# Silu order, late queries and 72-row keys and values in an attention and feed-forward kernel

## The chip, the cores and the metric

The kernel runs on one core of a Trainium2 chip. Its time is the device time of one execution in microseconds; the median of ten runs stands for a kernel. A profile is of one execution, and its times count from the start of that execution's span.

## What is computed

Eight batches of attention with pooled keys and values, then a feed-forward layer with silu over all 4608 rows:

```
k_p = k.reshape(B, H, Sp, 8, D).mean(axis=3)      # B=8, H=8, Sp=72, D=64
v_p = v.reshape(B, H, Sp, 8, D).mean(axis=3)
attn = softmax(q @ k_p.T / sqrt(D))               # q has 576 rows for each head
x = (attn @ v_p) as 4608 rows of 512
h = x @ w_in                                      # 512 x 2048
out = (h * sigmoid(h)) @ w_out                    # 2048 x 512
```

## The kernel before

The loop at L788 walks over nine tiles t of 512 rows. Each tile has a first product, `up` (x by w_in, with silu into `h_T`), and a second one: `down` for tile 0, `down_quarters` for the others. The attention of batch a = t + 1 is laid between the matmuls of tile t, so that PE always has work.

What is laid where is written by hand. `spread` (L417) counts the steps of a product and runs a list of fillers, each due at a step; `f_up` and `f_down` are the lists of the two products. A filler's instructions take their place in each engine's queue at that moment, and every engine runs its queue in order. DMAs are issued in three queues: SP (output stores and the first half of each later key and value load), POOL (weights, queries, and loads that cast or add), and ACT (a few at the start and the end).

**Tiles 1 to 8** make both products with fewer multiplications: seven products of quarter matrices instead of eight. In `up` this is done for two units of four column groups (`UNITS`, L428), the rest being plain (`plain`, L537). `stage` (L502) does one product of a unit: product 2 goes into PSUM bank P and is copied by ACT to `r_sb` (L505); product 5 goes into Q and DVE adds `r_sb` (L508, `rr_sb`); product 1 goes into R and gives `t_sb` (L511); products 4 and 3 add into P and Q and ACT takes their silu; products 7 and 6 add into P and Q, DVE adds `t_sb` to make `c_sb` 0 and 1 (L520, L524), and ACT takes their silu (L496). "s" in an item stands for the silu of `c_sb` 1, and that of `c_sb` 0 follows product 7 directly (L521). The order of units is the string in `items`. A plain group goes through three PSUM banks with the tag mm. In `down_quarters` the sums of quarters of `h_T` are made by DVE (`hidden_sum`, L611) into five tiles `h_sum`, and those of `w_out` into `w_sum` (`weight_sum`, L629, in tiles 0 and 1).

**Keys and values** come in two ways. For batches 0 to 2 the 576 rows of a batch (8 heads by 72 positions, each of 8 by 64 numbers) lie in 128 rows by slots of 128 (`load_slots`, L251). `slot_sums` (L269) adds the eight parts on DVE; since a head's 72 rows then straddle slots, PE puts them in place by selection matmuls (`select_k` L289, `select_v` L305: 24 for keys and 12 for values of a batch), and `copy_k` and `copy_v` take them out of PSUM. Batch 2 is loaded in two halves, the second added by the DMA. From batch 3 on, keys and values lie in 72 rows with the heads side by side: `load_one` (L175, SP) loads one half, `load_rest` (L181, POOL) adds the other, `pool_k` (L199) and `pool_v` (L211) add up on DVE (L188, L193), and `k_transpose` (L217) turns the keys with four transposes on PE and one copy on ACT.

**Queries** are loaded by POOL (`load_q`, L129): one DMA for a batch, but eight of 144 KB for the last batch. `q_transpose` (L150) turns them on DVE. `scores`, `denominators` and `numerators` (L343 to L408) are the attention itself; `numerators` needs the values `vp`.

Of the kernel before, what the change touches and what calls it, by code (L numbers as in the profile page):

```python
# [27 lines left out]
FP32 = mybir.dt.float32  # L28
# [8 lines left out]
def kernel(  # L37
# [9 lines left out]
    nc = tc.nc  # L47
# [43 lines left out]
    def ps_tile(shape, dtype, tag, name):  # L91
# [12 lines left out]

    h_sum = {
        n: singles.tile([128, KQ, NQ], BF16, name=f"h_sum{n}") for n in (1, 2, 5, 6, 7)
    }
    o_sb = [singles.tile([128, 2, d_model], FP32, name=f"o_sb{n}") for n in range(2)]
# [65 lines left out]

    def load_one(b, name):  # L175
        st = batches.setdefault(b, {})
        raw = raw_tile(f"{name}_raw", H)
        load_rows(nc.sync, raw, source(b, name)[:, :, :PH])
        st[f"{name}_raw"] = raw

    def load_rest(b, name):  # L181
# [5 lines left out]
    def add_halves(raw):  # L187
        nc.vector.tensor_add(  # L188
            out=raw[:, :, : 2 * D], in0=raw[:, :, : 2 * D], in1=raw[:, :, 2 * D :]
        )  # L190
# [59 lines left out]

    def load_slots(eng, b, name, i0, i1, half=None):  # L251
        es = slice(0, RE) if half is None else slice(half * RE // 2, (half + 1) * RE // 2)
        src = (k if name == "k" else v)[b].rearrange("h (sp p) d -> (h sp) (p d)", p=POOL)
        src = src[:, es]
        how = dict(accum_op=ALU.add) if half else {}
        tiles = row_tiles[name]
        w = es.stop - es.start
        if i0 == SLOTS:
            eng.dma_start(
                out=tiles[1][:REST, SLOTS - SA, :w], in_=src[128 * SLOTS :], **how  # L260
            )
        else:
            j = i0 // SA
            eng.dma_start(
                out=tiles[j][:, i0 - SA * j : i1 - SA * j, :w],
                in_=src[128 * i0 : 128 * i1].rearrange("(i r) e -> r i e", r=128), **how
            )

    def slot_sums(name, j, halves=False):  # L269
        raw = row_tiles[name][j]  # L270
        dst = rows5[name][:, SA:] if j else rows5[name][:, :SA]
        w = RE // 4 if halves else RE // 2
        while w > D:
            nc.vector.tensor_add(  # L274
                out=raw[..., :w], in0=raw[..., :w], in1=raw[..., w : 2 * w]
            )
            w //= 2
        nc.vector.tensor_add(out=dst, in0=raw[..., :D], in1=raw[..., D : 2 * D])
# [192 lines left out]
    def up(t, fillers, items):  # L471
        step = spread(
            fillers,
            sum(
                KF if len(it) == 3 else 2 * len(it[1].strip("s")) for it in items
            ),
# [25 lines left out]
        def stage(y, n):  # L502
# [3 lines left out]
            elif n == "5":  # L506
                product(y, 5, "Q", True)
                tt(out=rr_sb, in0=ps["Q"], in1=r_sb, op=ALU.add)  # L508
            elif n == "1":
                product(y, 1, "R", True)  # L510
                tt(out=t_sb, in0=ps["R"], in1=rr_sb, op=ALU.subtract)  # L511
            elif n == "4":
                product(y, 4, "P", False)
                hidden(y, 1, 0, ps["P"])
            elif n == "3":
                product(y, 3, "Q", False)
                hidden(y, 0, 1, ps["Q"])
            elif n == "7":
                product(y, 7, "P", False)
                tt(out=c_sb[0], in0=ps["P"], in1=t_sb, op=ALU.add)  # L520
                hidden(y, 0, 0, c_sb[0])  # L521
            elif n == "6":
                product(y, 6, "Q", False)
                tt(out=c_sb[1], in0=ps["Q"], in1=t_sb, op=ALU.add)  # L524
            else:
                hidden(y, 1, 1, c_sb[1])
# [243 lines left out]
    warm_up(2)  # L770
    load_slots(nc.gpsimd, 1, "k", 0, 3)
    load_slots(nc.gpsimd, 1, "k", 3, 4)
    load_slots(nc.gpsimd, 1, "k", 4, 5)
    load_q(1)
    load_w_in(1536, d_ff)
    for c in range(3):
        load_w_out(c)
    load_slots(nc.gpsimd, 1, "v", 0, 3)
    load_slots(nc.gpsimd, 1, "v", 3, 4)
    load_slots(nc.gpsimd, 1, "v", 4, 5)  # L780
    load_w_out(3)

    def load_half_2(name, half):
        for i0, i1 in ((0, SA), (SA, SLOTS), (SLOTS, SLOTS + 1)):
            load_slots(nc.gpsimd, 2, name, i0, i1, half)

    visits = [third(n) for n in range(3)]
    for t in range(NT):  # L788
# [11 lines left out]
        else:  # L800
            G = lambda *gs: [(g, 0, NTT) for g in gs]
            if t == 1:
                items = (
                    G(12, 13, 14, 15) + [(0, "251")] + G(8) + [(0, "43")] + G(9)
                    + [(0, "76")] + G(10) + [(0, "s")] + G(11, 0, 1, 2, 3)
                )
            else:
                items = (
                    G(12, 13) + [(0, "251")] + G(14) + [(0, "43")] + G(15) + [(0, "76")]
                    + [(1, "2")] + [(0, "s")] + [(1, "51")] + G(0) + [(1, "43")] + G(1)  # L810
                    + [(1, "76")] + G(2) + [(1, "s")] + G(3)
                )
# [108 lines left out]
```

The softmax here doesn't subtract the row's maximum and nothing guards it: scores larger than these inputs give would overflow.

## Time and profile before

| | |
|---|---|
| median of ten runs | 288.08 us (287.63 to 289.61) |
| the profiled execution | 288.15 us |
| its span | 286.2 us |
| clock granted to TensorE | 1.00 |
| DMA, whole span | 37.70 MB |

How to read the profile: PE is the matmul array, PEld its weight loads, DVE VectorE, ACT ScalarE, POOL GpSimd, SP the sync engine. A line of the timeline gives the start, how long the merged instructions took, the engine, the line in the kernel, the operation, what it writes and reads, and how many were merged. A bracket at its end is the idle time of that engine before it and what ended it. PE's intervals overlap, since matmuls are pipelined: the distance between starts tells what one costs. In the table by stretch each engine has its busy time and, in brackets, its instructions; the last two columns are the mean share of the 16 DMA queues that was busy, and GB/s. The trace also holds, for every DMA, the sixteen times at which its engines reported that their share had landed.

### The profile page before, as it was taken

The numbers are of one execution on the slowest core, as the hardware profiler recorded it, in microseconds if no ns is written. First come the engines' busy times: TensorE is split into PE (matmuls) and PEld (weight loads), VectorE is DVE, ScalarE is ACT, GpSimd is POOL, SyncE is SP. The second block draws the span as 40 slices with busy tenths as digits, with TensorE's granted clock in tenths as the row PEclk, the third lists the DMA queues.
The fourth block names the chain that finished last, engine by engine and source line by source line (L and its number), as shares of the span: only waits on it lengthen the run. The fifth ranks groups of instructions, "written<-read, shape, count | busy, mean of one in ns | idle before, by whom it ended". The sixth has DMA issues, their size and how long they took to land.

```text
span 286.2 us, 6919 instructions
## 1 busy us (share of the span) xinstructions
PE 278.4 (97%) x2773; PEld 195.4 (68%) x2793; DVE 225.5 (79%) x403; ACT 183.3 (64%) x359; POOL 52.2 (18%) x68
## 2 busy tenths in 40 slices
PE   8989999999999999999999999999999999999995
PEld 3448544566777677767888876687667867786684
DVE  4986845889879896989697969886988786836773
ACT  1677666568566875687658857794779558325700
POOL 8754217501020012001020108003000000000000
PEclk9999999999999999999999999999999999999999
DMA  7999999893668485973789487968930032005004
GB/s 213 279 274 220 226 309 176 215 205 61 136 92 197 111 106 106 143 196 59 153 144 221 57 118 103 165 128 159 158 84 0 2 83 66 2 8 140 1 3 147
DMA packets 35296, 37.70 MB, mean 132 GB/s; under 512 B 9952, under 2 KB 27616, under 8 KB 35264
## 3 DMA queue, kind: packets, MB, share of 16 engines
q0 software_dynamic: 21760, 20.86, 42.9%
q1 hardware_dynamic: 12928, 15.48, 22.2%
q10 hardware_dynamic: 576, 0.92, 0.9%
q8 instruction: 22, 0.36, 0.6%
q14 instruction: 10, 0.08, 0.1%
HBM read 36.70 MB, written 9.44 MB: 161 GB/s over the span
## 4 chain that ended last, share of the span: by engine, by line
PE 87%; DVE 6%; DMA 2%; ACT 2%; issue 2%; SPq 0%; DVEq 0%
PE hp_ps L546 23%; PE o_psP L654 15%; PE o_psQ L654 14%; PE u_psQ L488 6%; PE u_psP L488 6%; PE o_psR L654 5%; PE sc_ps L351 4%; PE o_ps L581 3%; PE nu_ps L395 2%; PE den_ps L369 2%; PE u_psR L488 2%; DMA raw<-in_k_dram 2%; DVE rr_sb L508 1%; PE warm_ps L703 1%; ACT r_sb L505 1%
## 5 line engine op out<-in xcount | busy, mean ns | idle before, releaser
L546 PE MATMUL hp_ps<-xT,w_in_sb 128*128 128x512 bf16 (+3 forms) x397 | 80.8, 339 | 1.3 <-ACT h_T L552 0.4
L552 ACT ACTIVATE h_T<-hp_ps 128x512 bf16<-128x512 f32 (+2 forms) x95 | 51.3, 545 | 27.3 <-PE hp_ps L546 26.3
L654 PEld LDWEIGHTS <-h_sum 128*128 128x128 bf16 x640 | 60.6, 98 | 11.9 <-issue 1.3
L546 PEld LDWEIGHTS <-w_in_sb 128*128 128x128 bf16 x412 | 39.3, 98 | 25.0 <-issue 1.4
L614 DVE TENSOR_TENSOR h_sum<-h_T 128x1024 bf16<-128x1024 bf16 (+1 forms) x72 | 50.9, 744 | 6.9 <-ACT h_T L552 6.9
L359 ACT ACTIVATE es<-sc_ps 72x384 bf16<-72x384 f32 (+1 forms) x100 | 39.0, 469 | 10.0 <-PE sc_ps L351 10.0
L488 PEld LDWEIGHTS <-w_sum 128*128 128x128 bf16 x300 | 29.2, 98 | 8.3 <-DVE x_sum L455 0.6
L654 PEld LDWEIGHTS <-h_T 128*128 128x128 bf16 x256 | 24.1, 98 | 4.4 <-issue 0.9
L496 ACT ACTIVATE h_T<-c_sb 128x512 bf16<-128x512 f32 x30 | 18.8, 628 | 11.7 <-DVE c_sb L520 11.7
L404 DVE TENSOR_TENSOR xT<-nu_ps,rec 128x384 bf16<-128x384 f32 (+1 forms) x50 | 24.0, 533 | 0.3
L378 ACT ACTIVATE lnd<-den_ps 128x384 f32<-128x384 f32 (+1 forms) x23 | 11.1, 483 | 20.2 <-PE den_ps L369 20.2
L153 DVE STREAM_TRANSPOSE qT<-q_bf 128x576 bf16<-128x576 bf16 x32 | 23.0, 753 | 0.0
L182 POOL DMA_DIRECT2D raw<-in_k_dram x5 | 7.0, 1404 | 67.9 <-DMA raw<-in_k_dram 41.0
L274 DVE TENSOR_TENSOR raw<-raw 128x384 f32<-128x384 f32 (+3 forms) x20 | 12.3, 617 | 7.1 <-DMA raw<-in_v_dram 3.8
L654 PE MATMUL o_psP<-w_out_sb,h_sum 128*128 128x256 bf16 x128 | 17.6, 273 | 0.0
L654 PE MATMUL o_psQ<-w_sum,h_sum 128*128 128x256 bf16 x128 | 16.7, 273 | 0.0
L654 PE MATMUL o_psQ<-w_out_sb,h_sum 128*128 128x256 bf16 x128 | 16.6, 273 | 0.0
L654 PE MATMUL o_psP<-w_sum,h_T 128*128 128x256 bf16 x128 | 16.5, 273 | 0.0
L654 PE MATMUL o_psQ<-w_sum,h_T 128*128 128x256 bf16 x128 | 16.5, 273 | 0.0
L488 PEld LDWEIGHTS <-w_in_sb 128*128 128x128 bf16 x120 | 11.7, 97 | 6.0 <-issue 2.0
L654 PE MATMUL o_psR<-w_sum,h_sum 128*128 128x256 bf16 x128 | 15.7, 274 | 0.0
L182 POOL DMA_DIRECT2D raw<-in_v_dram x5 | 6.9, 1389 | 47.1 <-DVE xT L404 23.7
(77 smaller groups left out, 422.6 us busy)
## 6 DMA issues: line engine op xcount, KB each, us to landing
out_dram<-o_sb SPq DMA_DIRECT2D x128, 64.0 KB, 2.9
q_bf<-in_q_dram POOLq DMA_DIRECT2D x6, 576.0 KB, 11.1
raw<-in_k_dram SPq DMA_DIRECT2D x6, 512.0 KB, 6.0
raw<-in_k_dram POOLq DMA_DIRECT2D x5, 576.0 KB, 10.0
raw<-in_v_dram POOLq DMA_DIRECT2D x5, 576.0 KB, 8.6
raw<-in_v_dram SPq DMA_DIRECT2D x5, 512.0 KB, 8.3
w_in_sb<-in_moe_w_in_dram POOLq DMA_DIRECT2D x8, 256.0 KB, 8.3
w_out_sb<-in_moe_w_out_dram POOLq DMA_DIRECT2D x4, 512.0 KB, 13.4
```

The costliest lines, as they stand in the source:

```text
L153: nc.vector.transpose(out=st["qT"][:, a, f * QF : (f + 1) * QF].rearrange("r i c p -> r (i c p)"), in_=st["q_bf"][:, a, f * n : (f + 1) * n],)
L182: nc.gpsimd.dma_start(out=batches[b][f"{name}_raw"], in_=source(b, name)[:, :, PH:], accum_op=ALU.add,)
L274: nc.vector.tensor_add(out=raw[..., :w], in0=raw[..., :w], in1=raw[..., w : 2 * w])
L351: nc.tensor.matmul(sc[s][:, cs], lhsT=kz[b % 2][rows, g, c, :], rhs=st["qT"][rows, g, i0:i1, c, :], start=(c == 0), stop=(c == 1),)
L359: nc.scalar.activation(es[:, s, :], sc[s], func=AF.Exp, scale=score_scale)
L404: nc.vector.tensor_mul(out=xT[:, 2 * g0 + c : 2 * (g0 + ng - 1) + c + 1 : 2, cols], in0=nu[c][:, :w].rearrange("r (g n) -> r g n", g=ng), ...
L488: nc.tensor.matmul(ps[bank][:, u, :], lhsT=w[:, kk, 128 * u : 128 * (u + 1)], rhs=x[:, kk, :], start=first and u == 0 and kk == 0, stop=kk ...
L496: nc.scalar.activation(h_T[:, g : g + 2, j * NQ : (j + 1) * NQ], src, func=AF.Silu)
L546: nc.tensor.matmul(hp_ps[:, r0:r1], lhsT=w_in_sb[:, kk, g * 128 : (g + 1) * 128], rhs=xT[:, kk, x0 : x0 + r1 - r0], start=(kk == 0), stop= ...
L552: nc.scalar.activation(h_T[:, g, n0 : n0 + n], hp_ps[:, :n], func=AF.Silu)
L614: nc.vector.tensor_tensor(out=h_sum[n][:, ks, :], in0=quarter(*a, ks), in1=quarter(*b, ks), op=op)
L654: nc.tensor.matmul(ps[b][:, c, :], lhsT=left(n, kt, c), rhs=W_OUT[n][:, kt, :], start=b not in begun, stop=kt == k1 - 1, skip_group_check= ...
```

## The change

Three things are changed.

1. The silu of `c_sb` 0 becomes an item of its own, "h". In tile 1 it stays where it was. In tiles 2 to 8 the first unit's "h" is placed after product 2 of the second unit, and so behind that product's `r_sb` copy on ACT.
2. The queries of the last batch are loaded at step 48 of tile 5's first product, not at step 1, and so behind the second key load of that batch on POOL.
3. Keys and values of batches 1 and 2 come in 72 rows by heads. Batch 1 is loaded whole, by one DMA each, into memory that is not in use yet: the keys where the `h_sum` tiles are (now one tile `h_sums`), the values in `w_sum`. One more sum on DVE (`add_early`) precedes `pool_k` and `pool_v`. Batch 2 is loaded like the later batches, but by POOL for both halves. The selections and slot sums of these batches go, and the due steps of sums, transposes and of tile 1's query transposes are new.

```diff
-    h_sum = {
-        n: singles.tile([128, KQ, NQ], BF16, name=f"h_sum{n}") for n in (1, 2, 5, 6, 7)
-    }
+    h_sums = singles.tile([128, 5, KQ, NQ], BF16, name="h_sums")
+    h_sum = {n: h_sums[:, i] for i, n in enumerate((1, 2, 5, 6, 7))}
...
+    early_raw = {
+        n: buf.rearrange("p a k c -> p (a k c)").bitcast(FP32)[:SP, : 2 * H * PH]
+        .rearrange("k (h e) -> k h e", h=H) for n, buf in (("k", h_sums), ("v", w_sum))
+    }
+
+    def load_early(b, name):
+        batches.setdefault(b, {})[f"{name}_raw"] = early_raw[name]
+        nc.gpsimd.dma_start(out=early_raw[name], in_=source(b, name))
+
+    def add_early(b, name):
+        raw = early_raw[name]
+        nc.vector.tensor_add(
+            out=raw[:, :, :PH], in0=raw[:, :, :PH], in1=raw[:, :, PH:]
+        )
...
                 product(y, 7, "P", False)
                 tt(out=c_sb[0], in0=ps["P"], in1=t_sb, op=ALU.add)
-                hidden(y, 0, 0, c_sb[0])
...
+            elif n == "h":
+                hidden(y, 0, 0, c_sb[0])
...
-    load_slots(nc.gpsimd, 1, "k", 0, 3)
-    load_slots(nc.gpsimd, 1, "k", 3, 4)
-    load_slots(nc.gpsimd, 1, "k", 4, 5)
+    load_early(1, "k")
     load_q(1)
     load_w_in(1536, d_ff)
     for c in range(3):
         load_w_out(c)
-    load_slots(nc.gpsimd, 1, "v", 0, 3)
-    load_slots(nc.gpsimd, 1, "v", 3, 4)
-    load_slots(nc.gpsimd, 1, "v", 4, 5)
+    load_early(1, "v")
     load_w_out(3)
...
-                    + [(0, "76")] + G(10) + [(0, "s")] + G(11, 0, 1, 2, 3)
+                    + [(0, "7h6")] + G(10) + [(0, "s")] + G(11, 0, 1, 2, 3)
...
-                    + [(1, "2")] + [(0, "s")] + [(1, "51")] + G(0) + [(1, "43")] + G(1)
-                    + [(1, "76")] + G(2) + [(1, "s")] + G(3)
+                    + [(1, "2")] + [(0, "hs")] + [(1, "51")] + G(0) + [(1, "43")] + G(1)
+                    + [(1, "7h6")] + G(2) + [(1, "s")] + G(3)
...
-            q_at = [15, 16, 17, 8] if t > 1 else [24, 25, 26, 2] if t else [82, 84, 86, 88]
+            q_at = [15, 16, 17, 8] if t > 1 else [25, 26, 27, 2] if t else [82, 84, 86, 88]
             if t == 0:
-                for j in range(2):
-                    f_up.append((44 + 8 * j, lambda j=j: slot_sums("k", j)))
-                    f_up.append((72 + 8 * j, lambda j=j: select_k(1, j)))
-                    f_up.append((72 + 8 * j, lambda j=j: copy_k(1, j)))
-                    f_down.append((20 + 10 * j, lambda j=j: slot_sums("v", j)))
-                    f_down.append((37 + 3 * j, lambda j=j: select_v(1, j, "at")))
-                    f_down.append((37 + 3 * j, lambda j=j: copy_v(1, j)))
-            elif t == 1:
-                for j in range(2):
-                    f_up.append((0, lambda j=j: slot_sums("k", j, halves=True)))
-                    f_up.append((22, lambda j=j: select_k(2, j)))
-                    f_up.append((23, lambda j=j: copy_k(2, j)))
-                    f_down.append((8, lambda j=j: slot_sums("v", j, halves=True)))
-                    f_down.append((40, lambda j=j: select_v(2, j, "at")))
-                    f_down.append((41, lambda j=j: copy_v(2, j)))
+                f_up.append((44, lambda: add_early(1, "k")))
+                for stage in range(2):
+                    f_up.append((52, lambda stage=stage: pool_k(1, stage)))
+                f_up.append((76, lambda: k_transpose(1)))
+                f_down.append((20, lambda: add_early(1, "v")))
+                f_down.append((30, lambda: pool_v(1)))
             else:
-                f_up.append((22, lambda: k_transpose(a)))
-                f_down.append((10, lambda: pool_v(a)))
+                f_up.append((40 if t == 1 else 22, lambda: k_transpose(a)))
+                if t == 1:
+                    for stage in range(2):
+                        f_up.append((24, lambda stage=stage: pool_k(2, stage)))
+                f_down.append((16 if t == 1 else 10, lambda: pool_v(a)))
...
-                f_down.append((0, lambda: load_half_2("k", 0)))
+                f_down.append((0, lambda: load_one(2, "k", nc.gpsimd)))
                 f_down.append((0, lambda: load_q(2)))
-                f_down.append((0, lambda: load_half_2("k", 1)))
-                for half in range(2):
-                    f_down.append((31, lambda half=half: load_half_2("v", half)))
+                f_down.append((0, lambda: load_rest(2, "k")))
+                f_down.append((31, lambda: load_one(2, "v", nc.gpsimd)))
+                f_down.append((31, lambda: load_rest(2, "v")))
...
-                f_up.append((1, lambda: load_q(a + 1)))
+                f_up.append((48 if a + 1 == B - 1 else 1, lambda: load_q(a + 1)))
```

More of the change, by code (lines that the diff above doesn't have):

```diff
@@ L173, in load_rows, with load_one @@
             eng.dma_start(out=out[r0:r1], in_=in_[r0:r1])
-    def load_one(b, name):
+    def load_one(b, name, eng=nc.sync):
         st = batches.setdefault(b, {})
         raw = raw_tile(f"{name}_raw", H)
-        load_rows(nc.sync, raw, source(b, name)[:, :, :PH])
+        if eng is nc.sync:
+            load_rows(eng, raw, source(b, name)[:, :, :PH])
+        else:
+            eng.dma_start(out=raw, in_=source(b, name)[:, :, :PH])
         st[f"{name}_raw"] = raw
+    early_raw = {
[10 more added lines that the diff above has]
+        )
     def load_rest(b, name):
@@ L188, in add_halves @@
         nc.vector.tensor_add(
-            out=raw[:, :, : 2 * D], in0=raw[:, :, : 2 * D], in1=raw[:, :, 2 * D :]
+            out=raw[:, :, : 2 * D], in0=raw[:, :, : 2 * D], in1=raw[:, :, 2 * D : 4 * D]
         )
@@ L248, with load_slots @@
     }
-    def load_slots(eng, b, name, i0, i1, half=None):
-        es = slice(0, RE) if half is None else slice(half * RE // 2, (half + 1) * RE // 2)
+    def load_slots(eng, b, name, i0, i1):
         src = (k if name == "k" else v)[b].rearrange("h (sp p) d -> (h sp) (p d)", p=POOL)
-        src = src[:, es]
-        how = dict(accum_op=ALU.add) if half else {}
         tiles = row_tiles[name]
-        w = es.stop - es.start
         if i0 == SLOTS:
-            eng.dma_start(
-                out=tiles[1][:REST, SLOTS - SA, :w], in_=src[128 * SLOTS :], **how
-            )
+            eng.dma_start(out=tiles[1][:REST, SLOTS - SA], in_=src[128 * SLOTS :])
         else:
@@ L264, in load_slots, with slot_sums @@
             eng.dma_start(
-                out=tiles[j][:, i0 - SA * j : i1 - SA * j, :w],
-                in_=src[128 * i0 : 128 * i1].rearrange("(i r) e -> r i e", r=128), **how
+                out=tiles[j][:, i0 - SA * j : i1 - SA * j],
+                in_=src[128 * i0 : 128 * i1].rearrange("(i r) e -> r i e", r=128),
             )
-    def slot_sums(name, j, halves=False):
+    def slot_sums(name, j):
         raw = row_tiles[name][j]
         dst = rows5[name][:, SA:] if j else rows5[name][:, :SA]
-        w = RE // 4 if halves else RE // 2
+        w = RE // 2
         while w > D:
@@ L474, in up @@
             sum(
-                KF if len(it) == 3 else 2 * len(it[1].strip("s")) for it in items
+                KF if len(it) == 3 else 2 * len(it[1].strip("hs")) for it in items
             ),
@@ L777 @@
         load_w_out(c)
-    load_slots(nc.gpsimd, 1, "v", 0, 3)
-    load_slots(nc.gpsimd, 1, "v", 3, 4)
-    load_slots(nc.gpsimd, 1, "v", 4, 5)
+    load_early(1, "v")
     load_w_out(3)
-    def load_half_2(name, half):
-        for i0, i1 in ((0, SA), (SA, SLOTS), (SLOTS, SLOTS + 1)):
-            load_slots(nc.gpsimd, 2, name, i0, i1, half)
     visits = [third(n) for n in range(3)]
```

## The prediction, made before the changed kernel ran

> **What bounds the kernel now.** I read the page's busy times and chain first, then busy time by stretch, then who TensorE waited for, then the timelines of the places that the diff touches.
>
> ```profile
> span 286.2 us, 6919 instructions
> PE 278.4 (97%) x2773; PEld 195.4 (68%) x2793; DVE 225.5 (79%) x403; ACT 183.3 (64%) x359; POOL 52.2 (18%) x68
> PE 87%; DVE 6%; DMA 2%; ACT 2%; issue 2%; SPq 0%; DVEq 0%
> ```
>
> TensorE (PE) is the bound: 97% busy and 87% of the chain. From start to start a 256-column matmul takes 108 ns and a 512-column one 216 ns nearly everywhere, so only two things shorten the kernel: fewer matmuls, or fewer stops. Busy time by stretch (PE, PEld, DVE, ACT, POOL, clock, DMA share, GB/s) shows where another resource is full beside it:
>
> ```profile
> 20.00:40.00 20.00, 19.90 (x191) 12.32 (x192) 13.48 (x28) 14.42 (x34) 7.03 (x11) 1.00 1.17 256
> 60.00:72.00 12.00, 12.00 (x100) 7.22 (x98) 11.84 (x26) 9.72 (x19) 1.43 (x1) 1.00 0.68 120
> ```
>
> To about 47 us the DMA queues are full (share over 1). From 60 to 72 us VectorE (DVE) is busy 11.84 of 12 us. These are the two places into which the third part of the change moves work.
>
> A stop that repeats, in the timeline of tile 2's second unit:
>
> ```profile
> 91.34 0.63 ACT L496 ACTIVATE h_T<-c_sb 128x512 bf16<-128x512 f32 x1 [1.07 <-DVE c_sb L520]
> 91.87 0.57 ACT L505 COPY r_sb<-u_psP 128x512 f32<-128x512 f32 x1
> 92.47 0.69 DVE L508 TENSOR_TENSOR rr_sb<-u_psQ,r_sb 128x512 f32<-128x512 f32 x1 [0.57 <-ACT r_sb L505]
> 93.22 0.60 PE L488 MATMUL u_psQ<-x_sum,w_in_sb 128*128 128x256 bf16 x4
> ```
>
> ScalarE (ACT) sits idle 1.07 us for c_sb, though the r_sb copy behind it is ready. DVE then waits 0.57 us for r_sb, and PE's product 3 starts only when rr_sb has been read out of its bank. Its neighbours are 108 ns apart, this pair 377.
>
> The selections of keys that the change removes, and the sums before them:
>
> ```profile
> 22.90 1.55 DVE L274 TENSOR_TENSOR raw<-raw 128x768 f32<-128x768 f32 x2
> 27.55 0.28 PE L296 MATMUL kz_ps<-shifts,k 128*32 128x72 bf16 x12
> 28.64 0.64 PE L296 MATMUL kz_ps<-shifts,k 128*32 128x72 bf16 x12
> ```
>
> [...]of the 16 landings of each L182 load (72 rows) about four come after 3.3 to 3.6 us where queues are quiet, the rest near 7; a 128-row load's 16 come within 0.5 us before 12 us, when nothing disturbs. [...]after a 72-row load the next query load also lands early on four engines. [...]The trace has 1196 ns for N = 1024[...]; I use an estimate of 2.25 us for N = 2048.
>
> **Part 1, silu behind the next unit's copy.** No instruction is added. After the move r_sb can run when product 2 ends (about 90.95), ending at 91.55. DVE finishes the second c_sb at 91.9 and can run rr_sb at once, to 92.5. PE wants product 3 at 92.95, so the stop goes with 0.45 us to spare. What is queued behind the moved silu on ACT (second silu, then the plain silu at 92.87) is no later, since ACT loses an idle gap. PE's excess at this pair is 0.27, 0.27, 0.29, 0.27, 0.29 us in tiles 2 to 6 and absent in 7 and 8: **minus 1.40 us.** Tile 1 keeps its order: zero.
>
> **Part 2, batch 7's queries.** Eight query DMAs of 144 KB go from before the second key load of batch 7 to behind it on POOL. Now they run from 173.5 to 185 us beside SP's 16 stores, which take 15.5 us there and 10 to 13.5 elsewhere. SP's first key load follows at 187.0, the second on POOL at 193.9, landing at 201.4, when DVE has waited 0.29 us; x_sum is late and PE stops 0.14 and 0.19 us at 204 and 206. With the stores quicker all that is about 4 us earlier: **minus 0.33 us.** Behind the moved DMAs: the eighth waits for its slot until the key load lands (about 197), then takes 5.4 us as now, 202.5; the transposes start at 207. If SP gains nothing the eighth lands at 206.8, still in time. The value load behind it lands near 206 to 210, needed at 217. Cover lost means DVE and PE waiting 1 to 4 us.
>
> **Part 3a, keys of batch 1.** Removed from PE: two groups of 12 selections. From the start of the matmul before to the one after, less one matmul, they cost 0.30 and 0.67 us. Added: four transposes, 0.13 by the L222 groups of later batches. Net minus 0.84. On DVE 3.25 us of sums become 2.25 + 1.93 (L188 and two L193, as at 83.05 to 84.98), 4.2 with start-up. The load is one DMA of the same 1.18 MB. Now w_in's sixth piece lands at 19.6 on most engines, 20.6 on the slowest, and the keys at 23.0 and 24.1. The same load on 12 engines takes 4/3 of 3.45 us, 4.6: it lands at 24.2, or 25.2 if the slowest engine is one of the twelve (three chances in four). I take 25.0, so kp is ready at 29.25. PE reaches step 76 at 27.84 (step 73 at 27.77, less the first selection 0.30, three steps of 95 ns, and one). PE is in order, so it stops 1.4 us (bounds 0.5 and 1.7). Net after the first product: **plus 0.56.** ACT's added kz copy (0.41 us) has ACT's idle time there and three PSUM banks to hide it.
>
> **3b, values of batch 1.** Selections off PE: 0.20 + 0.44 = minus 0.64. The values land now at 40.6; the keys' load makes that 0.9 later, and 4/3 of their own 3.84 us 1.3: I estimate 42.8, so vp is ready at 47.0 (2.25 + 1.20 + 0.69 on DVE), while PE wants it at 47.07 + 0.56 - 0.64 = 47.0. The last w_out piece moves from 42.6 to about 44.8, wanted at about 44.8. Both just hold. **Sum for tile 0: about minus 0.1.**
>
> **3c, keys of batch 2.** PE: minus 0.99 + 0.13. But DVE has the sums now in slack and loses them to a full stretch:
>
> ```profile
> 57.70 0.69 DVE L508 TENSOR_TENSOR rr_sb<-u_psQ,r_sb 128x512 f32<-128x512 f32 x1 [1.27 <-ACT r_sb L505]
> 59.53 2.09 DVE L153 STREAM_TRANSPOSE qT<-q_bf 128x576 bf16<-128x576 bf16 x3
> 68.80 2.49 DVE L614 TENSOR_TENSOR h_sum<-h_T 128x1024 bf16<-128x1024 bf16 x4
> 69.55 1.05 PE L654 MATMUL o_psP<-w_out_sb,h_sum 128*128 128x256 bf16 x8
> ```
>
> The slot sums stood before rr_sb, where DVE then waited 1.27 us. pool_k now stands behind t_sb: plus 1.93, minus 0.43 (the two kz copies), minus a gap of 0.16. From there DVE has no gap until the first low h_sum, done at 69.45; PE uses it at 69.55. DVE gets there 1.34 us later, PE would be there 0.86 earlier: PE stops some 2.1 us in sum (part of it already when the plain silu of G10 stands behind the late c_sb on ACT and a bank stays full). This step comes out at plus 1.25 against now, not minus 0.86; with tile 0's lead of 0.1: **plus 1.15.**
>
> **3d, values of batch 2.** PE minus 0.62. DVE does less (1.88 for 1.50 + 0.74). vp is ready about 0.8 us before PE asks. **Running sum plus 0.55.** The keys of batch 3 can enter their buffer only after pool_k, at 61 and not 56.4 us; landing near 78, wanted at 83.
>
> **Sum.** 0.55 - 1.40 - 0.33 = minus 1.2 us. The profiled execution took 288.15 us (span 286.2 and 1.95 around it), 0.07 over the median of 288.08: **286.9 us.**
>
> **Rivals.** *A, DVE's tail in tile 1 costs nothing* (its sums fit the slack I call gone): 3c is minus 0.86 and the time 284.8. For it: DVE idles before rr_sb. Against: pool_k's place is behind that idle time. *B, slower: the early loads are late.* Now these loads move as packets of 4096 bytes, 18 to an engine in 3.45 us: 159 ns and a gap of 33 each. If the 72-row form goes in packets of 2048 (84 to 96 ns in the first key load), 48 on each of 12 engines take 6.2 us where I assume 4.6. Keys land at 26.6 and PE stops 3.0 us; values land at 46.0, vp is ready at 50.2, wanted at 48.6. Tile 0 is then plus 3.1, and the time 288.15 + 3.1 + 1.25 - 0.62 - 1.73 = 290.1. Slower than before begins where the keys land after about 26 us. Against: the rows of one head adjoin in DRAM in both forms. *C, the silu move frees nothing* because product 3 waits for another thing: 288.3; against it, the 0.57 us idle on DVE has r_sb as its end.
>
> **How the numbers follow.** Main case 0.66, 286.9 with 286.0 to 287.8; A 0.13; B 0.13; C 0.08. About 0.2%, 0.58 us, is what a measurement can tell from no change: faster is under 287.5, slower over 288.66. Faster: 0.54 of the main case and A, 0.67. Same: 0.12 of the main case, C's 0.06, 0.02 of B, 0.20. Slower: 0.11 of B and 0.02 of C, 0.13. The range takes in half of A and ends just over C: 284.9 to 288.7.
>
> **What would show it.** Right: no excess on PE at product 3 of the second unit in tiles 2 to 6; no DVE wait for keys near 201; PE waiting for kp near 28 us; PE waiting for c_sb's bank or h_sum at the start of tile 1's second product. Wrong: keys landing before 24 or after 26 us, or DVE with idle time between t_sb and the low h_sum of tile 1.

## The result: slower by 2%

| | before | after |
|---|---|---|
| median of the runs | 288.39 us (32 runs) | 293.96 us (293.66 to 295.82, 9 runs) |
| ratio to before | | 1.0196, 95% interval 1.0176 to 1.0215 |
| span of the profiled execution | 286.2 us | 292.3 us |
| clock granted to TensorE | 1.00 | 0.988 |

The forecast of 286.9 us (284.9 to 288.7) missed, and on the wrong side.

### The profile after

Of the page: its span, PE's busy time, the clock in 40 slices, and the chain that ended last.

```profile
span 292.3 us, 6752 instructions
PE 278.4 (95%) x2709; PEld 194.7 (67%) x2729; DVE 225.3 (77%) x387; ACT 184.5 (63%) x361; POOL 44.5 (15%) x56
PEclk9999689999999999999999999999999999999999
PE 72%; DMA 16%; DVE 8%; issue 1%; POOL 1%; ACT 0%; SPq 0%; DVEq 0%; POOLq 0%
```

PE has 64 instructions fewer than before and yet the same 278.4 us of busy time; transfers have gone from 2% to 16% of the chain; and two slices, between 29 and 44 us, have a lower clock. All three point at the start of the kernel. The same two stretches as in the prediction, with the same columns:

```profile
20.00:40.00 20.00, 15.37 (x112) 10.12 (x112) 13.18 (x23) 9.71 (x25) 3.88 (x5) 0.83 1.16 212
60.00:72.00 12.00, 10.87 (x67) 6.28 (x67) 9.04 (x19) 7.90 (x15) 2.14 (x2) 1.00 0.72 156
```

From 20 to 40 us PE works 15.37 us where it worked 19.90. The DMA share is as full as before (1.16 for 1.17), but what it moves has fallen from 256 to 212 GB/s. The second line no longer covers the same work, since everything there comes 7 us later.

To see where the time goes, I laid the start of every product on PE beside that of before:

| PE begins | before | after | difference |
|---|---|---|---|
| tile 0, second product | 34.20 | 40.86 | +6.65 |
| tile 1, first product | 52.72 | 59.64 | +6.92 |
| tile 1, second product | 67.13 | 74.82 | +7.69 |
| tile 2, first product | 83.69 | 91.19 | +7.49 |
| tile 4, second product | 156.40 | 163.39 | +6.99 |
| last matmul of the kernel | 282.62 | 288.73 | +6.11 |

So tile 0 costs 6.92 us (predicted minus 0.1), tile 1 costs 0.57 (predicted plus 0.63), and tiles 2 to 8 give back 1.38 (predicted 1.73). Only tile 0 is wrong, and by 7 us.

DVE's timeline of tile 0 (the bracket is the idle time before and what ended it):

```profile
28.29 2.29 DVE L194 TENSOR_TENSOR h_sums<-h_sums 72x2048 f32<-72x2048 f32 x1 [5.36 <-DMA h_sums<-in_k_dram]
49.66 2.29 DVE L194 TENSOR_TENSOR w_sum<-w_sum 72x2048 f32<-72x2048 f32 x1 [11.06 <-DMA w_sum<-in_v_dram]
53.24 0.69 DVE L210 TENSOR_TENSOR vp<-w_sum 72x512 bf16<-72x512 f32 x1
```

And PE's:

```profile
32.34 0.64 PE L239 MATMUL kT_ps<-shifts,kp 72*128 72x72 bf16 x4 [4.38 <-DVE kp L210]
51.49 2.10 PE L593 MATMUL o_ps<-w_out_sb,h_T 128*128 128x512 bf16 x9 [0.46 <-DMA w_out_sb<-in_moe_w_out_dram]
53.98 0.51 PE L406 MATMUL nu_ps<-es,vp 72*32 72x192 bf16 x16
```

The keys land at 28.27 us (before 24.06) and the values at 49.64 (before 40.57). DVE waits for both. PE stops 4.38 us at the transposes of the keys, and for 6.83 us from near the end of that stop on (31.47 to 38.29) the granted clock is 0.5, which costs another 3 us (half of the 5.95 us that are left of it when PE goes on at 32.34). The values make little show in PE's idle time, because after such a delay PE arrives late itself. But the numerators start at 53.98, as soon as vp is there.

Landings, from the trace: of the keys' sixteen shares four come at 20.2 to 20.9 us, twelve at 26.5 to 28.3. I read this as twelve engines carrying the rows, the number that the prediction took; it was an estimate from the 72-row loads of before, whose landings have the same four ahead of the rest (197.3 to 197.5 us, the twelve 200.6 to 201.4, in the load issued on POOL at 193.94). A 64-row load of before, issued on SP at 125.44 us, has all sixteen landings from 129.7 to 130.3, so I count sixteen engines for 64 rows. What was not foreseen: the packets of 4096 bytes in this load took 312 ns in the median. In the stretch of the values' load, from 32 to 49 us, which takes in some packets of batch 2's keys, it was 319 ns. Before, both had a median of 159.

The two other parts did what they were to do. Tile 2's second unit after (before, these lines had 1.07 us of ACT idle and 0.57 of DVE idle in brackets):

```profile
98.93 0.59 ACT L516 COPY r_sb<-u_psP 128x512 f32<-128x512 f32 x1 [0.77 <-PE u_psP L499]
99.41 1.15 ACT L507 ACTIVATE h_T<-c_sb 128x512 bf16<-128x512 f32 x2
99.78 0.67 DVE L519 TENSOR_TENSOR rr_sb<-u_psQ,r_sb 128x512 f32<-128x512 f32 x1
100.41 0.60 PE L499 MATMUL u_psP<-x_sum,w_in_sb 128*128 128x256 bf16 x4
100.85 0.60 PE L499 MATMUL u_psQ<-x_sum,w_in_sb 128*128 128x256 bf16 x4
```

r_sb's copy now ends at about 99.5 and DVE has no gap before rr_sb. Product 3 (the one into u_psQ) starts 0.44 us after product 4, which is what four matmuls 108 ns apart take; before, it was 0.71 us (92.51 to 93.22).

### The profile page after: what moved, and what is told of

Same layout as the page of the kernel before. It is cut to its first block, busy times and chain, and to the rows that moved or that the text cites. A ratio compares the mean times of both kernels' runs of the same rounds, so it can differ in the third digit from the quotient of the medians.

```text
span 292.3 us, 6752 instructions
## 1 busy us (share of the span) xinstructions
PE 278.4 (95%) x2709; PEld 194.7 (67%) x2729; DVE 225.3 (77%) x387; ACT 184.5 (63%) x361; POOL 44.5 (15%) x56
## 4 chain that ended last, share of the span: by engine, by line
PE 72%; DMA 16%; DVE 8%; issue 1%; POOL 1%; ACT 0%; SPq 0%; DVEq 0%; POOLq 0%
PE hp_ps L558 17%; PE o_psP L666 15%; PE o_psQ L666 14%; DMA w_sum<-in_v_dram 10%; PE u_psQ L499 6%; PE u_psP L499 6%; PE o_psR L666 5%; DMA w_in_sb<-in_moe_w_in_dram 3%; PE sc_ps L362 3%; DMA raw<-in_v_dram 3%; DVE w_sum L644 2%; PE u_psR L499 2%; PE nu_ps L406 2%; PE den_ps L380 2%; DMA out_dram<-o_sb 1%
## 5 line engine op out<-in xcount | busy, mean ns | idle before, releaser
L558 PE MATMUL hp_ps<-xT,w_in_sb 128*128 128x512 bf16 (+3 forms) x397 | 83.5, 347 | 2.5 <-ACT h_T L564 1.5
L666 PEld LDWEIGHTS <-h_sums 128*128 128x128 bf16 x640 | 60.6, 98 | 12.3 <-issue 1.3
L564 ACT ACTIVATE h_T<-hp_ps 128x512 bf16<-128x512 f32 (+2 forms) x95 | 51.2, 546 | 27.1 <-PE hp_ps L558 25.6
L558 PEld LDWEIGHTS <-w_in_sb 128*128 128x128 bf16 x412 | 40.5, 100 | 27.8 <-issue 5.3
L626 DVE TENSOR_TENSOR h_sums<-h_T 128x1024 bf16<-128x1024 bf16 (+1 forms) x72 | 50.8, 742 | 6.9 <-ACT h_T L564 6.9
L666 PE MATMUL o_psP<-w_out_sb,h_sums 128*128 128x256 bf16 x128 | 17.6, 273 | 0.4 <-DVE h_sums L626 0.4
L666 PE MATMUL o_psQ<-w_sum,h_sums 128*128 128x256 bf16 x128 | 16.7, 273 | 0.0
L666 PE MATMUL o_psQ<-w_out_sb,h_sums 128*128 128x256 bf16 x128 | 16.6, 273 | 0.0
L666 PE MATMUL o_psR<-w_sum,h_sums 128*128 128x256 bf16 x128 | 15.5, 273 | 0.0
L666 PE MATMUL o_psP<-w_sum,h_sums 128*128 128x256 bf16 x128 | 15.4, 273 | 0.0
L531 DVE TENSOR_TENSOR c_sb<-u_psP,t_sb 128x512 f32<-128x512 f32 x15 | 10.1, 675 | 6.9 <-PE u_psP L499 3.6
```

The costliest lines, as they stand in the source:

```text
L558: nc.tensor.matmul(hp_ps[:, r0:r1], lhsT=w_in_sb[:, kk, g * 128 : (g + 1) * 128], rhs=xT[:, kk, x0 : x0 + r1 - r0], start=(kk == 0), stop= ...
L564: nc.scalar.activation(h_T[:, g, n0 : n0 + n], hp_ps[:, :n], func=AF.Silu)
L626: nc.vector.tensor_tensor(out=h_sum[n][:, ks, :], in0=quarter(*a, ks), in1=quarter(*b, ks), op=op)
L666: nc.tensor.matmul(ps[b][:, c, :], lhsT=left(n, kt, c), rhs=W_OUT[n][:, kt, :], start=b not in begun, stop=kt == k1 - 1, skip_group_check= ...
```

## The experiments

Theory at first: the late landing of batch 1's two early loads is the whole loss (and the half clock follows from it). Rivals: DVE's tail in tile 1, the half clock by itself, the length of the queue. Differences "on PE" below are starts of products in the profiled execution against before. One caution on them: executions begin tile 0's first product up to 1.06 us apart, with nothing changed ahead of it (17.11 us in before, 18.17 in the second run of p12), and that shift stays in every later start. Counted from that product the first two tiles repeat closely. To the begin of tile 1 it is 35.61 us in before and in the six runs that leave batch 1 in slots (slots1, p1, p12 and the rest), and 42.58 in after, so tile 0's loss is 6.97. Tiles 2 to 8 repeat only to about 1 us; sections 1 and 2 show why.

### 1. Take the early loads out, together and one by one

```diff
-    load_early(1, "k")          # slots1, v72
+    load_slots(nc.gpsimd, 1, "k", 0, 3) ... (3, 4), (4, 5)
-    load_early(1, "v")          # slots1, k72
+    load_slots(nc.gpsimd, 1, "v", 0, 3) ... (3, 4), (4, 5)
```

with the slot sums and selections of that tensor put back at their old steps. slots1 does it for both:

> The changed kernel with keys and values of batch 1 back in slots of 128 rows; batch 2 in 72 rows, the silu order and the late queries stay. Theory A (the two early 72-row loads land late and cost everything in tile 0): tile 0 is as before, tile 1 loses 0.6 us to DVE, tiles 2 to 8 gain 1.4 to 1.7, so about 287.3 us, 1.1 under before. Theory B (something else in the change costs too: the merged h_sums tile, batch 2's loads or the moved queries): 290 or more.

Measured: ratio 0.9972 (0.9951 to 0.9992). Tile 0 is at +0.03 on PE, so its whole loss is gone. In tile 1 the delay of 0.6 stays; the lines show DVE, and PE's two stops:

```profile
57.72 0.69 DVE L519 TENSOR_TENSOR rr_sb<-u_psQ,r_sb 128x512 f32<-128x512 f32 x1 [2.79 <-ACT r_sb L516]
65.21 2.89 PE L558 MATMUL hp_ps<-xT,w_in_sb 128*128 128x512 bf16 x12 [1.12 <-ACT h_T L564]
70.05 2.49 DVE L626 TENSOR_TENSOR h_sums<-h_T 128x1024 bf16<-128x1024 bf16 x4
70.80 1.05 PE L666 MATMUL o_psP<-w_out_sb,h_sums 128*128 128x256 bf16 x8 [0.38 <-DVE h_sums L626]
```

DVE idles 2.79 us before rr_sb (before: 1.27), since the key sums that stood there are now behind it; its h_sums come 1.25 us later than before, and PE's product starts at 70.80 where the prediction had 69.55 plus 1.25, also 70.80. Tiles 2 to 8 give back only 0.75 us, where 1.4 to 1.7 was expected: DVE waits for late keys near 113, 143 and 172 us, 1.3 us together, and PE stops behind it. Which batches' keys come late differs between executions (v72: near 116 and 176 us, 1.9 us together; k72: none).

k72 keeps only the keys' early load:

> The changed kernel with only the values of batch 1 back in slots; its keys still by the early load in 72 rows. Theory C (the keys' wait of 4.4 us on PE and the half clock after it are the cost): 294, like the changed kernel. Theory D (the late values set the end of tile 0, keys alone matter little): values land near 45 and the time is 289 or less.

Measured: 1.0118 (1.0062 to 1.0175), 291.66 us, between the two forecasts; span end +3.21, keys landed at 27.34.

```profile
31.42 0.64 PE L239 MATMUL kT_ps<-shifts,kp 72*128 72x72 bf16 x4 [3.18 <-DVE kp L210]
```

A stop of 3.18 us, then 3.41 us at half clock (from 31.6 us), together +4.57 at the second product. v72 keeps only the values' early load:

> The changed kernel with only the keys of batch 1 back in slots; its values still by the early load in 72 rows. Values should land near 45.5 and not 49.6 us, vp be ready near 49.8, PE wait some 3.4 us for it. Without a half clock: 290.2. If PE's clock is halved after that wait as it was after the keys': up to 293.5. Theory C (only the keys matter): 287.5.

Measured: 1.0095 (1.0062 to 1.0128), 291.00 us, end +3.00; tile 1 begins +2.59 late. The values land at 44.8 us, and it is not they that stop PE but the last w_out piece, queued behind them and landed at 47.42:

```profile
47.46 2.10 PE L593 MATMUL o_ps<-w_out_sb,h_T 128*128 128x512 bf16 x9 [2.86 <-DMA w_out_sb<-in_moe_w_out_dram]
```

In tile 0 itself, from its first product to the begin of tile 1, the keys' early load costs 4.34 us and the values' 2.38, together 6.72 of the 6.97 in after. Over the whole span each costs about 3.2 us against slots1; that the two come out alike there is made by tiles 2 to 8. What the trace pointed at is confirmed by taking it away.

### 2. Parts 1 and 2 alone

```diff
-                product(y, 7, "P", False); tt(c_sb[0], ...); hidden(y, 0, 0, c_sb[0])
+                product(y, 7, "P", False); tt(c_sb[0], ...)    # hidden(...) is item "h"
-                f_up.append((1, lambda: load_q(a + 1)))        # p12, not p1
+                f_up.append((48 if a + 1 == B - 1 else 1, lambda: load_q(a + 1)))
```

p12 has both on the kernel before, p1 only the first; p12 ran twice.

> The kernel before with the silu order and the late queries alone. My prediction's terms give minus 1.40 and minus 0.33: about 1.7 under before, 286.7. If the silu move frees nothing, 288.1.

> The kernel before with the silu order alone. The prediction's part 1 gives minus 1.40 us: end of span 284.8 to 285.0, ratio 0.995, and tiles 2 to 6 each 0.27 to 0.29 us shorter. With the late queries as well it was minus 1.4 in the profiled run and 0.9936: if the late queries gave their 0.33, this one gives about minus 1.05 to minus 1.4 and keeps PE's two stops near 204 and 206 us; if it gives minus 1.4 with those stops kept, the late queries gave nothing.

> The kernel before with silu order and late queries, again, beside the next one: 0.9925 to 0.9950.

Measured: p12 0.9936 (0.9912 to 0.9961) and 0.9910 (0.9877 to 0.9943), p1 0.9943 (0.9925 to 0.9962). From tile 1 to the end PE gains 1.52 us in p1, and 1.52 and 2.19 in the two runs of p12, where I had 1.40 and 1.73. p1 still has DVE waiting 0.28 us for the keys of batch 7 near 201 us, and neither run of p12 has such a wait: the late queries do what they were to do, but their third of a microsecond isn't resolved by the times.

That p1 and one run of p12 gain the same, and the other run more, has another reason: a wait for the keys of batch 5 near 142 us, which neither part touches and which differs between executions. The lines are of before (the first two), p1 (the next two) and the first run of p12; the second run of p12 has neither wait.

```profile
142.29 1.22 DVE L188 TENSOR_TENSOR raw<-raw 72x1024 f32<-72x1024 f32 x1 [0.42 <-DMA raw<-in_k_dram]
201.44 1.22 DVE L188 TENSOR_TENSOR raw<-raw 72x1024 f32<-72x1024 f32 x1 [0.29 <-DMA raw<-in_k_dram]
142.20 1.22 DVE L188 TENSOR_TENSOR raw<-raw 72x1024 f32<-72x1024 f32 x1 [0.31 <-DMA raw<-in_k_dram]
200.80 1.22 DVE L188 TENSOR_TENSOR raw<-raw 72x1024 f32<-72x1024 f32 x1 [0.28 <-DMA raw<-in_k_dram]
142.14 1.22 DVE L188 TENSOR_TENSOR raw<-raw 72x1024 f32<-72x1024 f32 x1 [0.66 <-DMA raw<-in_k_dram]
```

PE's two stops behind the first of these waits, near 145 and 147 us, sum to 0.43 us in before, 0.32 in p1, 0.67 and 0.00 in the two runs of p12. With these stops as they were before, the gains would be 1.41 us in p1 and 1.75 and 1.76 in p12.

### 3. Why the loads are late: loads by themselves

The micro kernels leave the whole computation out and write zeros. The first issues one form of load at a time, each when the one before has landed (the loads of 128 rows and on SP's queue are left out here):

```diff
+ gpsimd.dma_start(out=buf[:72],    in_=rows[b])        # 72 rows, partitions 0 to 71
+ gpsimd.dma_start(out=buf[:64],    in_=rows[b, :64])   # 64 rows, 0 to 63
+ gpsimd.dma_start(out=buf[32:96],  in_=rows[b, :64])   # 64 rows, 32 to 95
+ gpsimd.dma_start(out=buf[32:104], in_=rows[b])        # 72 rows, 32 to 103
```

> Loads alone, one after the other: the kernel computes nothing and writes zeros. The same 2 KB rows of keys are loaded as 128 rows of 4; 72 rows of 8 from partition 0; 64 rows of 8 from partition 0; 64 rows of 8 from partition 32; 72 rows of 8 from partition 32; and 72 rows on SP's queue. Theory P[...]: packets of 4096 bytes take 159 ns for 128 rows, 310 or more for 64 and 72 rows from partition 0, and near 160 for 64 rows from partition 32, with the same number of engines. Theory E (12 engines of 16): 64 rows from either place take as long as 128 rows of 4, some 3 us less than the 72. Theory R (the source rows): all forms with heads side by side take 310.

| form | packet of 4096 bytes, median | issue to last landing |
|---|---|---|
| 128 rows of 4 pieces | 159 ns | 5.6 to 6.2 us |
| 64 rows from partition 32 | 159 ns | 6.1 us |
| 64 rows from partition 0 | 311 to 318 ns | 7.3 to 7.5 us |
| 72 rows from partition 0 | 277 to 287 ns | 9.7 to 9.9 us |
| 72 rows from partition 32 | 159 ns, 5% over 323 | 8.1 us |
| 72 rows from partition 0, SP's queue | none; packets of 2048 bytes, 146 to 156 ns | 9.3 to 9.4 us |

The loads of 72 rows move 1.18 MB, the others 1.05. Theory P (the partitions into which the rows go set the packet time): its forecasts hold, except that 72 rows from partition 0 take 277 to 287 ns and not 310 or more. Theories R and E fall: with heads side by side in both, 64 rows are fast in one place and slow in the other. The number of rows costs time besides: 72 rows from partition 32 have fast packets and take 2.0 us longer than 64 (8.1 for 6.1), for an eighth more bytes. That this comes from twelve engines in place of sixteen is my reading.

The pair of 64 rows is clean: the same rows out of DRAM, the same 272 packets (256 of them of 4096 bytes), and only the partitions differ. It takes 311 ns into partitions 0 to 63, and 159 where half of the rows lie in each half of the partitions. The two have a ratio of 1.96; what lies behind it, no run here shows.

I took it for a matter of the lower half of the partitions. That was half of it, as the next run in the kernel showed.

### 4. The same in the kernel

shift32 is the changed kernel with both early loads on partitions 32 to 103:

```diff
-        nc.gpsimd.dma_start(out=early_raw[name], in_=source(b, name))
+        nc.gpsimd.dma_start(out=early_raw[name][32 : 32 + SP], in_=source(b, name))
...                                                  # partitions 0 to 31 are zeroed
```

> The changed kernel with one thing different: the two early loads of batch 1 land on partitions 32 to 103 and not 0 to 71 (partitions 0 to 31 of the two buffers are zeroed in the first microseconds). The kernel computes with partitions 0 to 71 as before, so batch 1's keys and values are moved by 32 rows and partly zero; every operation keeps its size and place. Theory P[...]: most packets near 160 ns and not 315, keys landed at 25 to 26 us (28.3 in the changed kernel), values at 43 to 45.5 (49.6), tile 0 longer by 1 to 3 us and not 6.7, 287.5 to 290. Rival, twelve of sixteen engines and the place in the queue are the cost whatever the partitions: keys at 28, values at 49, 293.5 to 294.5.

Measured: 1.0151 (1.0095 to 1.0207), packets still at about 315 ns, tile 1 begins +6.53 (0.40 of it there already at tile 0's first product).

```profile
27.25 2.29 DVE L194 TENSOR_TENSOR h_sums<-h_sums 72x2048 f32<-72x2048 f32 x1 [3.88 <-DMA h_sums<-in_k_dram]
47.40 2.29 DVE L194 TENSOR_TENSOR w_sum<-w_sum 72x2048 f32<-72x2048 f32 x1 [9.82 <-DMA w_sum<-in_v_dram]
```

Nearer to the rival than to my theory: keys at 27.2 and values at 47.4. split goes the other way: partitions 0 to 71 again, but as 64 rows (sixteen engines, as counted above) and 8.

```diff
-        nc.gpsimd.dma_start(out=early_raw[name], in_=source(b, name))
+        load_rows(nc.gpsimd, early_raw[name], source(b, name))   # rows 0 to 63, 64 to 71
```

> The changed kernel with each early load as two DMAs, 64 rows and 8, so that the 64 use all 16 engines. Theory P: packets still take about 310 ns; keys land near 26.5, values near 46, time about 290.5. Theory E: packets of 159 ns, keys at 24, values at 41, about 287.5.

Measured: 1.0212 (1.0164 to 1.0260), packets at 343 ns for the keys and near 350 for the values. So theory E is out; theory P had the packets, but not the landings: the last of the keys came at 29.56 and of the values at 49.11. PE's stop for kp is even longer:

```profile
33.71 0.64 PE L239 MATMUL kT_ps<-shifts,kp 72*128 72x72 bf16 x4 [5.60 <-DVE kp L210]
```

So neither cure helps alone. shift32_64 has both: 64 rows on partitions 32 to 95, and 8 on 96 to 103.

```diff
+        for r0, r1 in ((0, 64), (64, SP)):
+            nc.gpsimd.dma_start(out=early_raw[name][32 + r0 : 32 + r1], in_=source(b, name)[r0:r1])
...                                                  # partitions 0 to 31 are zeroed
```

> As the run with the early loads on partitions 32 to 103 (batch 1's keys and values moved by 32 rows and partly zero, everything else in size and place as in the changed kernel), but each load is split into 64 rows, on all sixteen engines and half in either half of the partitions, and 8 rows. Theory Q[...]: packets near 160 ns, keys landed at 24.5 to 26, values at 42 to 44.5, tile 0 longer by 0 to 2.5 us, 286.5 to 289.5. Rival, partitions do not matter in place (something in the kernel's traffic makes these packets slow): packets over 300 ns as with the split on partitions 0 to 71, keys at 29, values at 48.5 to 49, 293.5 to 295.

Measured: 1.0018 (0.9993 to 1.0043); packets at 159 ns in both loads; keys landed at 25.6 (64 rows) and 26.9 (8 rows), values at 43.4 and 43.7; no half clock. DVE and then PE:

```profile
25.65 2.29 DVE L195 TENSOR_TENSOR h_sums<-h_sums 72x2048 f32<-72x2048 f32 x1 [2.13 <-DMA h_sums<-in_k_dram]
43.46 2.29 DVE L195 TENSOR_TENSOR w_sum<-w_sum 72x2048 f32<-72x2048 f32 x1 [7.48 <-DMA w_sum<-in_v_dram]
```

```profile
29.70 0.57 PE L240 MATMUL kT_ps<-shifts,kp 72*128 72x72 bf16 x4 [1.16 <-DVE kp L211]
46.15 2.10 PE L594 MATMUL o_ps<-w_out_sb,h_T 128*128 128x512 bf16 x9 [0.49 <-DMA w_out_sb<-in_moe_w_out_dram]
```

Tile 1 begins +1.29 late, 0.54 of it there already at tile 0's first product: tile 0 has lost 0.75 us. One reservation: DVE here waits for the 64 rows alone, since the 8 lie beyond the partitions that it reads. With them it would start 1.3 us later for the keys and 0.3 for the values, so I estimate that some 5 to 6 us of the 6.97 are gone by the place and the split of the load, with every other operation as in the changed kernel. This layout cannot be used as it stands, since the sums need the rows from partition 0. It shows that the place and the split of the load together bring the packets back to 159 ns; the place alone left them at about 315 (shift32), the split alone at 343 to 350. That the split acts through the number of engines is my reading.

micro2 asks what company does. Each form has a query load ahead of it and weights and queries behind it, without waits between:

> Loads alone; nothing of the reference is computed, the output is zeros. Six groups: a query load, then one form of key load, two weight pieces and a query load queued behind it on the same queue without a wait between: a 128 rows of four pieces, b 72 rows from partition 0, c 72 rows from partition 32, d 64 rows from partition 0, e 64 rows from partition 32, f 64 rows from partition 64. Theory Q: 4096-byte packets near 160 ns in a and e; over 300 in b, d and f (f is the other half alone, so it is one half that crowds, not the lower one); c over 250 too, with neighbours, though it had a median of 159 when alone. Rival, only the lower half is slow: f near 160. Rival, company does not matter: c at 159.

Measured medians: a (128 rows) 159 ns, b (72 from 0) 293, c (72 from 32) near 270, d (64 from 0) near 335, e (64 from 32) 159, f (64 from 64) 324. The packets of c and d overlap in time, so these two are rough. f settles that the lower half is nothing special: one half alone, either one, is slow. And c differs from its 159 ns alone: with 72 rows across both halves, company brings slow packets back (near 270); with 64 (e) it doesn't (159). Why, no run here shows.

### 5. Is it the half clock?

warm is the changed kernel with 20 matmuls without use (512 columns) ahead of the transposes, to keep PE busy over its wait:

```diff
+                f_up.append((76, keep_warm))
                 f_up.append((76, lambda: k_transpose(1)))
```

> The changed kernel with 20 dummy matmuls of 512 columns on PE ahead of the transposes of batch 1's keys, in the time in which PE waits for them, so that its clock isn't halved. If the half clock is a cost of its own: 2 to 3 us less, 291 to 292. If the values' landing near 49.6 sets the end of tile 0 whatever PE does before: 293.5 to 294.

Measured: 1.0218 (1.0179 to 1.0256). The second product of tile 0 starts at +3.80 and not +6.65, so the half clock there is really gone, yet tile 1 starts at +7.27:

```profile
28.18 4.48 PE L720 MATMUL warm_ps<-warm 128*128 128x512 bf16 x20
50.78 3.45 PE L593 MATMUL o_ps<-w_out_sb,h_T 128*128 128x512 bf16 x9 [2.60 <-DMA w_out_sb<-in_moe_w_out_dram]
```

PE waits 2.60 us for w_out, landed at 50.74, and then runs at half clock (9 matmuls in 3.45 us, not 2.10). In the changed kernel the values and w_out behind them set the end of tile 0, so giving back the time at half clock alone is worth nothing. Taking the keys' early load away does help, since the values then land earlier too (44.8 us in v72).

### 6. A version that beats both

In slots1, pool_k(2) moves from step 24 of tile 1's first product to step 0, into the place where DVE was seen to idle:

```diff
-                        f_up.append((24, lambda stage=stage: pool_k(2, stage)))
+                        f_up.append((0, lambda stage=stage: pool_k(2, stage)))
```

> Slots for batch 1 as in slots1, and the sums of batch 2's keys due at step 0 of tile 1, ahead of rr_sb, where DVE stood idle 2.8 us in slots1. If DVE's place of these sums is the cost in tile 1: tile 1's second product starts 0.8 us earlier and the time is 287.2 or less. If the keys' landing at 55.6 makes rr_sb late instead: no gain or 0.5 us slower than slots1.

> The changed kernel with batch 1 in slots again and batch 2's key sums at the start of tile 1's first product, again, beside the one above. Batch 2 in 72 rows takes 0.86 + 0.62 us of selections off PE; if VectorE no longer pays for it in tile 1 this is 1.0 to 1.5 us below silu order and late queries alone: 0.988 to 0.991. If it is no faster than those alone, the late key loads of batch 2 and 3 (x_sum late) give the selections back.

Measured: 0.9923 (0.9896 to 0.9950), and 0.9891 (0.9855 to 0.9928) in the repeat, beside p12's 0.9910 on the same chip.

```profile
55.39 1.22 DVE L205 TENSOR_TENSOR raw<-raw 72x1024 f32<-72x1024 f32 x1 [0.43 <-DMA raw<-in_k_dram]
57.76 0.69 DVE L519 TENSOR_TENSOR rr_sb<-u_psQ,r_sb 128x512 f32<-128x512 f32 x1 [0.35 <-ACT r_sb L516]
68.90 1.05 PE L666 MATMUL o_psP<-w_out_sb,h_sums 128*128 128x256 bf16 x8
```

The key sums fill the idle time before rr_sb (0.35 us where slots1 had 2.79), PE doesn't stop at its product, and tile 1 comes out 1.34 us shorter than before, of the 1.48 that the removed selections are worth. Over the run PE ends 2.92 us earlier than before in the repeat, from which the lines are, and 1.41 in the first run, whose tile 0 began 1.01 us late. That this is better than p12 by itself is likely from the trace, but the medians are 0.55 us apart, where 1.0 to 1.5 was expected, and the intervals of the two overlap.

## Why the prediction was wrong, step by step

- **3a, keys of batch 1: the step that failed.** "The same load on 12 engines takes 4/3 of 3.45 us, 4.6: it lands at 24.2, or 25.2": twelve engines fits the landings (four at 20.2 to 20.9 us, twelve at 26.5 to 28.3), but the time per packet was carried over from a 128-row load, 159 ns, and it was 312. The keys landed at 28.27, not 25.0, and PE stopped 4.38 us, not 1.4. With the packet time as I assumed it (shift32_64) 64 rows land at 25.6 and all 72 at 26.9, in an execution that was 0.54 us late from the start, and PE, which waits for the 64 alone, stops 1.16 us. The first sum on DVE, 2.25 us by my estimate, took 2.29; a straight line through the sums of 512 and 1024 columns in before (0.69 and 1.20 us) gives 2.21. The half clock behind the stop, 3 us, had no term at all; section 5 shows that in this kernel it cost nothing in the end, since the values came later still.
- **3b, values: the same error.** "4/3 of their own 3.84 us" and 42.8 us for the landing: it was 49.64, and the last w_out piece behind it came at 51.45, not 44.8. These two set the end of tile 0. Where the packets took 159 ns the values landed at 43.7 and vp was ready at 47.7, which less the late start of 0.54 is 43.2 and 47.2 (47.0 foreseen). "Both just hold" then failed by 0.49 us for w_out. So the sum for tile 0, minus 0.1, would have been near plus 0.75 on its own assumption, up to 2 with the 8 rows (an estimate), and was plus 6.9.
- **Rival B** had the place, the sign and the point from which it decides (keys after about 26 us), but the wrong cause: packets of 2048 bytes. They stayed at 4096 and took twice as long. It got a chance of 0.13 because I looked only at packet size, against which there was evidence. The destination, the partitions of the 72 rows, was not looked at. B's own price, tile 0 plus 3.1, was less than half of what came.
- **3c and 3d, batch 2: right,** in size and in mechanism. Plus 0.63 foreseen for tile 1, 0.57 in after and 0.59 in slots1; the product at 70.80, as worked out; and of PE's stop 1.12 us is a wait for ACT's silu of a plain group, as the prediction had it. Rival A falls. That DVE's place was the cause is shown by moving it (section 6).
- **Part 1: right,** minus 1.40 foreseen, 1.52 measured alone, 1.41 without the chance part in the wait near 142 us. Rival C falls. **Part 2: right** in mechanism; its 0.33 is below what the times resolve, and the traces have 0.34 to 0.35 (section 2). In after tiles 2 to 8 gave 1.38 of the 1.73 foreseen: it has stops of 0.15 to 0.21 us of its own near 94, 96, 123 and 125 us, where late key loads make x_sum late. Such waits vary between executions, so the closeness of any one sum over these tiles is in part luck.
- One reading in the prediction is a little off, without effect: the 128-row loads before 12 us have their landings within 0.6 us (11.38 to 11.97), not 0.5.
- **The range:** it went up to 288.7, as far as rival C, and left B's 290.1 outside with a chance of 0.13. The two landings were the least known numbers of the sum and no bound for a slower packet was taken in.

## What to carry over

The time of these loads was not their bytes by a packet time of another load: ask which engines carry a load, and which partitions they write. Moving a load from 128 rows to 72 from partition 0 cost here a factor of two in packet time (312 ns for 159) and, as I read the landings (four of sixteen some 6 us ahead), a quarter of the engines, and what was queued behind it was late too (the last w_out piece at 51.45 us for 42.6). With two late loads in one queue, shortening what the first one's wait costs (warm) only brought out the second (tile 1 at +7.27 for +6.92), while taking the first one's delay away (v72) brought the second forward as well (44.8 us for 49.64). So price the last to land, and then ask whether a stop costs clock as well.

## What the runs showed of the hardware that was not expected

- Packets of 4096 bytes into 64 partitions of one half: 311 to 318 ns from partition 0 (micro), 324 from partition 64 (micro2); 159 ns where 64 rows lie across both halves.
- 72 rows across both halves: 159 ns alone (micro), about 270 to 315 ns between other loads (micro2, shift32).
- From tile 0's first product to the begin of tile 1 seven executions without the early loads took 35.61 us each, within 0.01; tile 1 took 31.55 to 31.56 us in eight with batch 2's sums at step 24. What varies is the time before that product and the waits for late keys in tiles 2 to 8.
- Half clock came with stops of 2.5 (shift32), 2.6 (warm), 3.2, 4.4 and 5.6 us and lasted 3.4 or 6.8 us, but not with stops of 2.86 (v72) and 2.90 (shift32). So the length of the stop alone doesn't decide.
- The trace's record of the clock explains the difference. In each trace the clock changes only at multiples of 3.413 us from the record's first entry: in after, which starts at 4.16, it is halved eight steps later, at 31.46, and in warm, from 5.76, thirteen steps later, at 50.13. Half clock followed steps in which PE was idle for 1.95 us (warm), 2.50 (shift32), 3.18 (k72) and 3.41 (after, split). It did not follow steps with 1.89 us idle (v72), or with 1.38 and 1.66, into which the end of a step cuts the stop of 2.90 (shift32). In these traces the idle time within one step tells the two groups apart; that they part near 1.9 us is my estimate from the 1.89 of v72 and the 1.95 of warm, and rough, since PE's ends are modelled.
